# Moving modulation vectors, row transforms and magnitude products to other places in a state-space plus token-mixer kernel

## The chip, the cores and the metric

The kernel runs on one core of a Trainium2 chip. The metric is the device time of one execution in microseconds (us): median 664.15 us of three runs, from 663.93 to 666.26. The engines are named as the profile names them: PE is TensorE (PEld its weight loads), DVE is VectorE, ACT is ScalarE, POOL is GpSimd, and SP is SyncE, whose queue issues nearly all DMAs.

## The reference

The input x is a matrix of 2048 tokens by 448 channels. A conditioning vector gives six modulation vectors of 448 numbers, and the block then does two things with them.

```python
mod = (silu(c) @ w_mod).reshape(1, 6, 1, -1)         # sa, ca, ga, sb, cb, gb
h = layernorm(x) * (1 + ca) + sa
# S4D: K[d, l] = 2 Re sum_n C[d, n] exp(A[d, n] dt[d] l),  256 complex states per channel
y = irfft(rfft(h, 4096) * rfft(K, 4096))[:2048] + h * D_skip
x = x + ga * y
h = layernorm(x) * (1 + cb) + sb
# token mixer over the 2048 tokens, 1792 hidden
x = x + gb * (w2.T @ gelu(w1.T @ h + b1) + b2)
```

## The kernel before, in words

**The kernel table.** The first half of the program makes K. The 448 channels are 28 groups of 16, and each group takes two steps, so that `s` runs from 0 to 55. The steps stand in seven sets of eight. A set begins with a window (`window`, `late_window`), in which ACT has its exponential table loaded, and goes on with eight sine steps (`st_step`). In the window, round `e` of eight rounds has ACT take two exponentials (`st_exp`, tile `mag`) of what PE wrote (`st_exponents`, tiles `xe` and `xg`, two buffers each), while PE writes the exponents of the next step of the set. In a step, PE writes the phases of step s+1 (`st_phase`, the same tiles); ACT takes two absolute values and four sines; POOL makes the two halves of `G` (lines 737 and 738); DVE makes the four quarters of `E` (lines 739, 740, 742, 743). Two steps later PE multiplies `G` and `E` into `kg` (`st_kgen`, line 764). The second half of `E` needs a magnitude product `m` (`st_mag2`, a small product `w` on line 712 and a large one on line 717), made by POOL. In the sets that begin at steps 8, 16 and 24 the window makes two of these products and the steps make the other six.

**Work that rides along.** In the same half the input is normalized and transformed. `u_rows` (32 calls) multiplies rows of x by a table into `pu` (line 591), and DVE scales the result (line 595) into `yt`, whose DMA goes to DRAM. `u_cols` (16 calls) reads that back, multiplies again (line 627), and DVE writes `uo` (line 631), whose DMA writes `us_d`. `modulation(k, half)` makes vector k of the six: the first half is four products of the loaded `w_mod` columns (line 537), copied out as `parts`; the second half sums over partitions (line 533) and is copied out as `mod`. `chains` is a generator of the parameter logarithms and angles of the channel groups 1 to 3; `more(n)` advances it n steps. `st_s1` transforms finished kernel columns (`y`, line 802), and from step 33 on `piece` multiplies spectra (`kx`, `vv`). `warm(n)` and `idle(n)` issue n bf16 products whose result nobody reads.

**What sets the order.** PE, ACT, DVE and POOL follow the order in which the code is written. Two lists, `dve` and `act`, hold results that wait to be copied out; `flush` empties them. Inside a step, `between` empties `dve` between the second and the third quarter of `E`, so that results asked for in step s are copied out in the middle of step s+1. SP follows the code as well up to step 8 (`first`); from there on the scheduler puts its DMAs in order. A queue works strictly in its order.

**Buffers.** The small PSUM tiles of tag `ms` (`pu`, `pm`, `y`, `kx`, `vv`) share three buffers, `E` has three, `gs` three, `yt` three. Steps 32 to 55 reuse the memory of the pools that are closed at step 32 (`early.close()`), among them that of `uo`.

**The second half.** After step 55 the spectra of the other 224 channels are multiplied, then the layer norm and the token mixer follow, whose products are written as three products of split fp32r numbers (`acc`, lines 1400 to 1402; `o`, lines 1563 to 1565).

Of the kernel before, what the change touches and what calls it, by code (L numbers as in the profile page):

```python
# [22 lines left out]
P = 128  # L23
# [209 lines left out]
def tile_adaln_s4d_mixer(ctx, tc, i, out):  # L233
# [19 lines left out]
    with ExitStack() as es:  # L253
# [99 lines left out]
        def wm_slot(k):  # L353
# [8 lines left out]
                wm_load(0, wm_slot(0)),  # L362
# [8 lines left out]
            12: lambda: wm_load(4, xt[0:PP, 0:4, 0:D]),  # L371
            13: lambda: wm_load(5, xt[0:PP, 4:8, 0:D]),
            14: lambda: wm_load(3, xt[0:PP, 8:12, 0:D]),
        }

# [145 lines left out]
        scb = qp.tile([PP, 4, 32], F32, name="scb")  # L521
        sums = qp.tile([P, P], F32, name="sums")
# [6 lines left out]
        def modulation(k, half):  # L529

            pm = pms.tile([P, D], F32, tag="ms", name="pm")
            if half:
                T.matmul(pm, sums, pmods.pop(k), start=True, stop=True)
                act.append(lambda: S.activation(mod[k], pm, AF.Copy, bias=1.0 if k in (1, 4) else 0.0))
                return
            for q in range(4):
                T.matmul(pm[32 * q : 32 * q + 32], scb[:, q], wms[k][:, q], start=True, stop=True)
            pmods[k] = qp.tile([P, D], F32, tag="parts", name="parts")
            act.append(lambda: S.copy(pmods[k], pm))
# [29 lines left out]
        yts, wurs, lent = {}, {}, []  # L569
# [6 lines left out]
        def u_rows(n):  # L576

            R, g = divmod(n, 4)
            gp, gl = divmod(g, 2)
            if gl == 0:  # L580
                pair = n // 2
                if pair in (2, 4):
                    E = gp_.tile([P, 2, GD, NJ], F32, tag="E", name="yE")
                    rooms = E.rearrange("p a g j -> p (a g j)")[:, 0 : 4 * D].rearrange("p (h g d) -> p h g d", h=2, g=2)
                    lent.extend(rooms[:, h] for h in range(2))
                yts[R, gp] = lent[pair - 2] if 2 <= pair < 5 else xp.tile([P, 2, D], F32, tag="yt", name="yt", bufs=3)
            if g == 0 and R < 6:
                u_table(R + 2)
            pm = pms.tile([P, D], F32, tag="ms", name="pu")
            p = slice(64 * gl, 64 * gl + 64)  # L590
            T.matmul(pm, wurs[R][p, gp], xt[p, 2 * R + gp], start=True, stop=True)  # L591

            def out():
                mean = means[:, gl, 2 * R + gp : 2 * R + gp + 1]
                stt(yts[R, gp][:, gl], pm, mean, mod[1], ALU.add, ALU.mult)
# [46 lines left out]
        mags, m2s, eg, phs = {}, {}, {}, {}  # L642
# [66 lines left out]
        def st_mag2(s):  # L709
            me = v32(mags[s][:, 0])  # L710
            w = wp.tile([P, GD], F32, tag="w", name="w")
            G.tensor_tensor(w[:, :, None], me[:, :, 31:32], me[:, :, 1:2], ALU.mult)
            if s in (3, 4, 5):
# [3 lines left out]
            G.tensor_tensor(m2, me, w[:, :, None].to_broadcast([P, GD, 32]), ALU.mult)  # L717
            m2s[s] = m2
# [322 lines left out]
        def more(n):  # L1041

            for _ in range(n):
                if next(rest, None) in ("logs", "end"):
                    return
# [5 lines left out]
        def some(f, it, n):  # L1051
            for _ in range(n):
                k = next(it, None)
                if k is not None:
                    f(k)

# [15 lines left out]
        def late_window(s):  # L1072

            flush(hold)
            for e in range(BATCH):
# [10 lines left out]
                elif e in (3, 5):  # L1086
                    piece(False, True)
                st_mag2(s + e)
# [3 lines left out]
        def window(s):  # L1092
            if s:
                aside.append(True)
            angle()
# [9 lines left out]
            for e in range(BATCH):  # L1105
# [11 lines left out]
                if s < 32:  # L1117
                    more(WPACE[s // 8][e])
                if s == 0 and e >= 4:
                    u_stats(e - 4)  # L1120
                if s == 8 and e in (3, 4):
                    modulation(0, e - 3)
                if s == 8 and e == 5:
# [9 lines left out]
                for k, e0 in ((4, 1), (5, 3), (3, 6)) if s == 16 else ():  # L1133
                    if e in (e0, e0 + 1):
                        modulation(k, e - e0)
# [12 lines left out]
                elif s and (e < 2 or s >= 32):  # L1148
# [15 lines left out]
        WPACE = [[0, 2, 2, 1, 1, 1, 1, 1], [2, 2, 2, 2, 1, 3, 3, 1], [4] * 7 + [9], [4] * 8]  # L1164
        pace = [2] * 5 + [3, 4, 4] + [2] * 24
        for s in range(NHALF):
# [24 lines left out]
            def between():  # L1191
# [4 lines left out]
                if s < len(pace):  # L1196
# [3 lines left out]
            if True:  # L1200
                if s < 32 and s % BATCH > 1:
                    st_kgen(s - 2)
                if s % BATCH == 1 or s < 24 and s % BATCH == 0:
                    warm(10)
# [4 lines left out]
                if s == 7:  # L1209
                    warm(10)  # L1210

# [14 lines left out]
            if s in (1, 2):  # L1226
                x_load(4 + 4 * s, 4, G)
            if s in (23, 31):
# [3 lines left out]
            if s + 2 < 32 and (s + 2) % BATCH > 1 and s + 2 > 5:  # L1232
# [7 lines left out]
            if 8 <= s < 16 and free:  # L1240
                some(u_rows, rows, 2 if s % 2 else 3)
# [9 lines left out]
            if 17 <= s < 32 and free:  # L1251
                some(u_cols, cols, 1)
# [344 lines left out]
```

## Time and profile before

| what | value |
|---|---|
| median of three runs | 664.15 us (663.93 to 666.26) |
| the profiled execution | 663.85 us |
| its span in the trace | 662.1 us |
| busy in the span | PE 612.3, DVE 443.0, ACT 439.9, POOL 269.5 us |
| granted clock, mean | 0.984 |
| DMA | 123.67 MB, 187 GB/s |

The profiled execution spends 1.75 us outside its span and lies 0.30 us below the median. A timeline row gives start, duration, engine, line and tiles, and in brackets the idle time just before it with what ended that. A row of the table by stretches gives, behind the stretch and its length, the busy time of PE, PEld, DVE, ACT and POOL with the number of instructions, then the granted clock, the DMA share and GB/s.

### The profile page before, as it was taken

What the parts mean: (1) busy time and instruction counts of PE and PEld (TensorE: products, weight loads), DVE (VectorE), ACT (ScalarE), POOL (GpSimd) and SP (SyncE); (2) the same over time, 40 slices, a digit from 0 to 9 for tenths busy, and PEclk for the clock granted to TensorE, in tenths of its full rate; (3) what the DMA queues carried; (4) which work ended last, traced back from release to release, by engine and by line L of the source; (5) the groups of instructions that cost most, each with busy time, mean ns of one, the idle gap of its engine ahead of it and who ended that gap; (6) DMA issues with size and microseconds to landing.
All of it is one profiled execution on the core that took longest, in us unless ns stands there. A gap on an engine that the chain in (4) does not pass through costs nothing.

```text
span 662.1 us, 19161 instructions
## 1 busy us (share of the span) xinstructions
PE 612.3 (92%) x7639; PEld 442.9 (67%) x7639; DVE 443.0 (67%) x853; ACT 439.9 (66%) x828; POOL 269.5 (41%) x351
## 2 busy tenths in 40 slices
PE   1878998999999999999888999999999999999997
PEld 0444555445455565656544577788999999999996
DVE  8989889689894887868655688777422553333331
ACT  5978888899989999999587678885222522222220
POOL 7785597588599788787563000000000000000000
PEclk9998999989999999999999899999999999999999
DMA  6595747598775557576787999946755275555530
GB/s 145 156 219 166 253 143 257 182 248 268 218 247 178 103 166 218 169 215 182 234 274 227 257 247 234 233 112 196 201 160 153 57 209 164 162 160 166 161 106 28
DMA packets 97858, 123.67 MB, mean 187 GB/s; under 512 B 13717, under 2 KB 79801, under 8 KB 97769
## 3 DMA queue, kind: packets, MB, share of 16 engines
q1 hardware_dynamic: 97032, 120.02, 64.2%
q0 software_dynamic: 736, 2.43, 1.5%
q8 instruction: 60, 0.98, 0.7%
q14 instruction: 30, 0.24, 0.1%
HBM read 88.33 MB, written 33.59 MB: 184 GB/s over the span
## 4 chain that ended last, share of the span: by engine, by line
PE 63%; DMA 11%; DVE 9%; ACT 7%; POOL 4%; issue 4%; SPq 3%; ACTq 0%; DVEq 0%; POOLq 0%
PE o L1563 7%; PE o L1565 7%; PE o L1564 7%; PE acc L1400 6%; PE acc L1401 6%; PE acc L1402 6%; PE xe L667 6%; PE kg L764 6%; DMA w<-in_B_w_dram 3%; PE xg L667 3%; DMA xt<-in_A_u_dram 3%; DMA v_d<-vt 3%; PE pu L591 2%; PE vv L895 2%; PE kx L872 2%
## 5 line engine op out<-in xcount | busy, mean ns | idle before, releaser
L218 ACT CAST whi<-w 128x896 fp32r<-128x896 f32 x64 | 59.7, 939 | 138.5 <-PE o L1564 82.7
L227 DVE TENSOR_TENSOR wlo<-w,whi 128x896 fp32r<-128x896 f32 x64 | 68.1, 1086 | 41.4 <-ACT whi L218 35.1
L737 POOL TENSOR_TENSOR G<-mag,gs 128x512 f32<-128x512 f32 x56 | 71.9, 1283 | 36.4 <-ACT gs L733 36.4
L1400 PE MATMUL acc<-h3h,whi 128*128 128x448 f32 x224 | 83.0, 371 | 1.7 <-ACT h3h L1467 0.9
L1401 PE MATMUL acc<-h3l,whi 128*128 128x448 f32 x224 | 81.4, 363 | 0.5 <-DVE h3l L1474 0.3
L1563 PE MATMUL o<-uh,whi 128*128 128x448 f32 x224 | 81.3, 363 | 0.0
L1565 PE MATMUL o<-uh,wlo 128*128 128x448 f32 x224 | 81.2, 362 | 0.0
L1402 PE MATMUL acc<-h3h,wlo 128*128 128x448 f32 x224 | 81.0, 361 | 0.0
L1564 PE MATMUL o<-ul,whi 128*128 128x448 f32 x224 | 80.6, 360 | 0.0
L764 PEld LDWEIGHTS kg<-E,G 128*32 128x32 f32 x3584 | 56.2, 114 | 33.1 <-issue 18.4
L738 POOL TENSOR_TENSOR G<-mag,gs 128x512 f32<-128x512 f32 x56 | 71.9, 1285 | 0.0
L764 PE MATMUL kg<-E,G 128*32 128x64 f32 x3584 | 65.9, 227 | 6.4 <-issue 4.2
L667 PE MATMUL xg<-tab,lph 64*128 64x512 f32 x112 | 62.0, 553 | 6.6 <-DVE E L743 4.3
L1568 DVE TENSOR_TENSOR y<-o,x 128x448 f32<-128x448 f32 x16 | 10.0, 624 | 79.0 <-PE o L1565 79.0
L667 PE MATMUL xe<-tab,lph 64*128 64x512 f32 x112 | 61.9, 553 | 0.3 <-issue 0.2
L717 POOL TENSOR_TENSOR m<-mag,w 128x512 f32<-128x512 f32 x53 | 55.8, 1053 | 4.2
L1400 PEld LDWEIGHTS acc<-h3h,whi 128*128 128x128 f32 x224 | 42.0, 188 | 14.8 <-issue 2.1
L729 ACT ACTIVATE ab<-xe 128x512 f32<-128x512 f32 x56 | 33.9, 604 | 16.3 <-PE xg L667 9.1
L1401 PEld LDWEIGHTS acc<-h3l,whi 128*128 128x128 f32 x224 | 42.0, 187 | 3.8 <-DVE h3l L1474 0.9
L1565 PEld LDWEIGHTS o<-uh,wlo 128*128 128x128 f32 x224 | 42.1, 188 | 3.4
L1402 PEld LDWEIGHTS acc<-h3h,wlo 128*128 128x128 f32 x224 | 42.0, 187 | 3.1
L1564 PEld LDWEIGHTS o<-ul,whi 128*128 128x128 f32 x224 | 41.9, 187 | 3.0
(257 smaller groups left out, 1399.1 us busy)
## 6 DMA issues: line engine op xcount, KB each, us to landing
w<-in_B_w_dram SPq DMA_DIRECT2D x64, 224.0 KB
w<-in_B_w_dram SPq DMA_DIRECT2D x32, 448.0 KB
yi<-yu_d SPq DMA_DIRECT2D x32, 224.0 KB
us_d<-uo SPq DMA_DIRECT2D x16, 448.0 KB
u<-us_d SPq DMA_DIRECT2D x64, 112.0 KB
v_d<-vt SPq DMA_DIRECT2D x32, 224.0 KB
vt<-v_d SPq DMA_DIRECT2D x14, 448.0 KB
yu_d<-yt SPq DMA_DIRECT2D x13, 448.0 KB
```

The lines of the kernel that those rows point to most:

```text
L218: self.nc.scalar.copy(hi, w)
L227: eng.tensor_tensor(lo, w, hi.bitcast(F32), ALU.subtract)
L667: T.matmul(out[k], lhs[r], rhs[r], start=start, stop=stop)
L737: G.tensor_tensor(Gt[:, 1], mg_, v32(sg), ALU.mult)
L738: G.tensor_tensor(Gt[:, 0], mg_, v32(cg_), ALU.mult)
L764: T.matmul(kg[32 * q : 32 * q + 32, m], Gt[:, c, d], E[:, c, d], start=h == 0 and c == 0 and m == 0, stop=h == 1 and c == 1, skip_group_ch ...
L1400: nc.tensor.matmul(acc[f], hi[:, fs], h3h[:, r], start=r == 0, stop=False)
L1401: nc.tensor.matmul(acc[f], hi[:, fs], h3l[:, r], start=False, stop=False)
L1402: nc.tensor.matmul(acc[f], lo[:, fs], h3h[:, r], start=False, stop=r == 15)
L1563: nc.tensor.matmul(o, hi[:, ks], uh[kh][:, k], start=kh == 0 and k == 0, stop=False)
L1564: nc.tensor.matmul(o, hi[:, ks], ul[kh][:, k], start=False, stop=False)
L1565: nc.tensor.matmul(o, lo[:, ks], uh[kh][:, k], start=False, stop=kh == 1 and k == 6)
```

## The change

1. **Modulation vectors.** Vector 0 is made in the window at step 16 and no more in the one at step 8; vectors 4, 3 and 5 are made in the windows at steps 32, 40 and 48 (`last_mods`) and no more in the one at step 16. Results of these last three are copied out by DVE, not by ACT. Their `w_mod` columns are loaded into a lent `E` buffer after steps 31, 38 and 46 (`wm_room`).
2. **Rows.** `u_rows` takes two rows a step in steps 9 to 15 (it was three and two in turn from step 8 on), and the last eight rows in the window at step 16 (it was five). For later `yt` tiles, rows of x that are done with are lent (`spare`), and no `E` buffer.
3. **Copies behind E.** `at_once` puts the copies of `u_rows` and `u_cols` behind the fourth quarter of `E` of the same step.
4. **Magnitude products.** The windows at steps 8 and 16 make four instead of two (`MSET`); one lent `E` buffer holds two of them (`rooms`).
5. **Chains.** In steps 8 to 31 the chain is advanced at the end of a step. The window at step 16 does not begin the third chain; step 16 does.
6. **Warming.** The ten products after step 7's phases go, and step 9 has five for ten.

```diff
@@ modulation loads
-                wm_load(0, wm_slot(0)),
...
-            12: lambda: wm_load(4, xt[0:PP, 0:4, 0:D]),
-            13: lambda: wm_load(5, xt[0:PP, 4:8, 0:D]),
-            14: lambda: wm_load(3, xt[0:PP, 8:12, 0:D]),
+            12: lambda: wm_load(0, xt[0:PP, 0:4, 0:D]),
         }
+        def wm_room(k):
+            E = gp_.tile([P, 2, GD, NJ], F32, tag="E", name="wE")
+            wm_load(k, E.rearrange("p a g j -> p (a g j)")[0:PP, 0 : 4 * D].rearrange("p (q d) -> p q d", q=4))
+        last_mods = {32: 4, 40: 3, 48: 5}
@@ modulation
+                if k > 2:
+                    dve.append(lambda: ts(mod[k], pm, one_more, None, ALU.add))
...
+            (dve if k > 2 else act).append(lambda: (V.tensor_copy if k > 2 else S.copy)(parts, pm))
@@ new
+        def at_once(f, it, n):
+            k = len(dve)
+            some(f, it, n)
+            for out in dve[k:]:
+                out()
+            del dve[k:]
@@ late_window, e of eight
+                if e in (4, 6):
+                    modulation(last_mods[s], (e - 4) // 2)
@@ window
+            if s in (8, 16):
+                E = gp_.tile([P, 2, GD, NJ], F32, tag="E", name="mE")
+                for k in range(2):
+                    rooms[s + k] = E[:, k].rearrange("p g j -> p (g j)")[:, 0:512].rearrange("p (d i) -> p d i", i=32)
...
-                    more(WPACE[s // 8][e])
+                    more(WPACE[s // 8][e], s != 16)
...
-                if s == 8 and e in (3, 4):
-                    modulation(0, e - 3)
-                if s == 8 and e == 5:
+                if s == 16 and e == 4:
                     G.tensor_tensor(mod[0], mod[0], mod[2], ALU.mult)
...
-                for k, e0 in ((4, 1), (5, 3), (3, 6)) if s == 16 else ():
-                    if e in (e0, e0 + 1):
-                        modulation(k, e - e0)
+                if s == 16 and e in (1, 2):
+                    modulation(0, e - 1)
+                if s == 32 and e in (4, 6):
+                    modulation(last_mods[s], (e - 4) // 2)
...
-                elif s and (e < 2 or s >= 32):
+                elif s and e < (BATCH if s >= 32 else MSET[s // BATCH]):
                     st_mag2(s + e)
...
+        MSET = [0, 4, 4, 2]
@@ steps
-                if s < len(pace):
+                if s < len(pace) and not 8 <= s < 32:
                     more(pace[s])
...
-                    warm(10)
+                    warm(5 if s == 9 else 10)
...
-                if s == 7:
-                    warm(10)
...
+            if s in (31, 38, 46):
+                wm_room(last_mods[s + BATCH - s % BATCH])
...
-            if s + 2 < 32 and (s + 2) % BATCH > 1 and s + 2 > 5:
+            if s + 2 < 32 and (s + 2) % BATCH >= max(2, MSET[s // BATCH]) and s + 2 > 5:
                 st_mag2(s + 2)
...
-            if 8 <= s < 16 and free:
-                some(u_rows, rows, 2 if s % 2 else 3)
+            if 8 < s < 16 and free:
+                at_once(u_rows, rows, 2)
...
-                some(u_cols, cols, 1)
+                at_once(u_cols, cols, 1)
+            if 8 <= s < 32 and s % BATCH != BATCH - 1:
+                more(pace[s])
```

The first place is POOL from the middle of the window at step 8 into the first step of its set. Before:

```order
L404 CAST hl<-s 128x256
L784 TENSOR_TENSOR ks<-ks,dsk 128x8
L406 TENSOR_TENSOR hl<-s,hl 128x256
L574 TENSOR_TENSOR wur<-wu,rs 128x256
L1125 TENSOR_TENSOR mod_104<-mod_104,mod_106 128x448
L574 TENSOR_TENSOR wur<-wu,rs 128x256
L737 TENSOR_TENSOR G<-mag,gs 128x512
L738 TENSOR_TENSOR G<-mag,gs 128x512
L712 TENSOR_TENSOR w<-mag 128x16
L717 TENSOR_TENSOR m_1359<-mag,w 128x512
```

The same place on POOL after the change:

```order
L408 CAST hl<-s 128x256
L724 TENSOR_TENSOR w<-mag 128x16
L731 TENSOR_TENSOR m_1129<-mag,w 128x512
L798 TENSOR_TENSOR ks<-ks,dsk 128x8
L410 TENSOR_TENSOR hl<-s,hl 128x256
L587 TENSOR_TENSOR wur<-wu,rs 128x256
L724 TENSOR_TENSOR w<-mag 128x16
L731 TENSOR_TENSOR m_1153<-mag,w 128x512
L587 TENSOR_TENSOR wur<-wu,rs 128x256
L751 TENSOR_TENSOR G<-mag,gs 128x512
L752 TENSOR_TENSOR G<-mag,gs 128x512
L751 TENSOR_TENSOR G<-mag,gs 128x512
```

Two products `m` with their `w` stand ahead of the first `G` of the set, the product of `mod` is gone from here, and the `G` of the second step follows that of the first without a product between them.

The second place is SP around step 31, ahead of the window at step 32. `u` is what the first spectra read, `lph` are the phase rows of later groups. Before:

```order
L634 DMA us_d<-uo 128x2x448
L653 DMA lph_141<-pars_59 32x256
L634 DMA us_d<-uo 128x2x448
L657 DMA lph_141<-pars_59 64x1x256
L828 DMA u<-us_d 32x2x448 x4
L841 DMA si<-in_SI_dram 128x512
```

After the change:

```order
L646 DMA us_d<-uo 128x2x448
L665 DMA lph_141<-pars_59 32x256
L669 DMA lph_141<-pars_59 64x1x256
L665 DMA lph_139<-pars_59 32x256
L669 DMA lph_139<-pars_59 64x1x256
L842 DMA u<-us_d 32x2x448
L341 DMA wE<-in_w_mod_dram 112x4x448
L842 DMA u<-us_d 32x2x448 x3
L855 DMA si<-in_SI_dram 128x512
```

The load of vector 4's columns (`wE`) stands behind the first load of `u`, and one `us_d` fewer and one more pair of `lph` loads stand ahead of it.

The third place is PE in the later rounds of the window at step 32; `lex` are the exponents of the set, `lph` the phases of its first step. Before:

```order
L667 MATMUL xe<-tab,lex_144 128x512
L667 MATMUL xg<-tab,lex_144 128x512
L667 MATMUL xe<-tab,lex_145 128x512
L667 MATMUL xg<-tab,lex_145 128x512
L667 MATMUL xe<-tab,lex_145 128x512
L667 MATMUL xg<-tab,lex_145 128x512
L667 MATMUL xe<-tab,lph_140 128x512
L667 MATMUL xg<-tab,lph_140 128x512
```

After the change:

```order
L679 MATMUL xe<-tab,lex_144 128x512
L679 MATMUL xg<-tab,lex_144 128x512
L545 MATMUL pm<-wE,scb 32x448 x4
L679 MATMUL xe<-tab,lex_145 128x512
L679 MATMUL xg<-tab,lex_145 128x512
L679 MATMUL xe<-tab,lex_145 128x512
L679 MATMUL xg<-tab,lex_145 128x512
L537 MATMUL pm<-parts,sums 128x448
L679 MATMUL xe<-tab,lph_140 128x512
L679 MATMUL xg<-tab,lph_140 128x512
```

The product that needs `wE` stands ahead of the exponents of the set's last two steps and of the first phases; the sum stands between those exponents and the phases.

More of the change, by code (lines that the diff above doesn't have):

```diff
@@ L520, in tile_adaln_s4d_mixer @@
         sc = qp.tile([PP, 4], F32, name="sc")
-        scb = qp.tile([PP, 4, 32], F32, name="scb")
-        sums = qp.tile([P, P], F32, name="sums")
+        scb = cg.tile([PP, 4, 32], F32, name="scb")
+        sums = cg.tile([P, P], F32, name="sums")
         G.memset(sums, 0.0)
@@ L533, in modulation @@
                 T.matmul(pm, sums, pmods.pop(k), start=True, stop=True)
-                act.append(lambda: S.activation(mod[k], pm, AF.Copy, bias=1.0 if k in (1, 4) else 0.0))
+                one_more = 1.0 if k in (1, 4) else 0.0
+                if k > 2:
+                    dve.append(lambda: ts(mod[k], pm, one_more, None, ALU.add))
+                else:
+                    act.append(lambda: S.activation(mod[k], pm, AF.Copy, bias=one_more))
                 return
@@ L537, in modulation @@
                 T.matmul(pm[32 * q : 32 * q + 32], scb[:, q], wms[k][:, q], start=True, stop=True)
-            pmods[k] = qp.tile([P, D], F32, tag="parts", name="parts")
-            act.append(lambda: S.copy(pmods[k], pm))
+            if k > 2:
+                parts = wp.tile([P, 512], F32, tag="ab", name="parts", bufs=1)[:, 0:D]
+            else:
+                parts = qp.tile([P, D], F32, tag="parts", name="parts")
+            pmods[k] = parts
+            (dve if k > 2 else act).append(lambda: (V.tensor_copy if k > 2 else S.copy)(parts, pm))
         mv = xp.tile([P, 16, 2], F32, name="mv")
@@ L567, in u_means @@
             dve.append(lambda: V.tensor_copy(means, pm))
-        yts, wurs, lent = {}, {}, []
+        yts, wurs = {}, {}
+        spare = {3: 0, 4: 1, 6: 2, 8: 3, 10: 4, 12: 5, 14: 6}
         def u_table(R):
@@ L581, in u_rows @@
                 pair = n // 2
[L582 to L586, printed above, removed]
+                if pair in spare:
+                    yts[R, gp] = xt[:, 2 * spare[pair] : 2 * spare[pair] + 2]
+                else:
+                    yts[R, gp] = xp.tile([P, 2, D], F32, tag="yt", name="yt", bufs=3)
             if g == 0 and R < 6:
@@ L639, in u_cols @@
                 u_load(p + 4)
-        mags, m2s, eg, phs = {}, {}, {}, {}
+        mags, m2s, eg, phs, rooms = {}, {}, {}, {}, {}
         v32 = lambda t: t.rearrange("p (d i) -> p d i", i=32)
@@ L712, in st_mag2 @@
             G.tensor_tensor(w[:, :, None], me[:, :, 31:32], me[:, :, 1:2], ALU.mult)
-            if s in (3, 4, 5):
+            if s in rooms:
+                m2 = rooms.pop(s)
+            elif s in (3, 4, 5):
                 m2 = v32(wm0.rearrange("p k d -> p (k d)")[:, -512 * (s - 2) :][:, 0:512])
@@ L1039, in tile_adaln_s4d_mixer, with more @@
         rest = chains()
-        def more(n):
+        ended = [False]
+        def more(n, begin=True):
+            if ended[0] and not begin:
+                return
             for _ in range(n):
-                if next(rest, None) in ("logs", "end"):
+                at = next(rest, None)
+                ended[0] = at == "end"
+                if at in ("logs", "end"):
                     return
@@ L1160, in window @@
                 S.activation(one, one, AF.Sin)
-        WPACE = [[0, 2, 2, 1, 1, 1, 1, 1], [2, 2, 2, 2, 1, 3, 3, 1], [4] * 7 + [9], [4] * 8]
+        MSET = [0, 4, 4, 2]
+        WPACE = [[0, 2, 2, 1, 1, 1, 1, 1], [2, 2, 2, 2, 1, 3, 1, 3], [4] * 7 + [9], [4] * 8]
         pace = [2] * 5 + [3, 4, 4] + [2] * 24
```

## The prediction

> **What bounds the kernel now.** I read the page, then cut the span at the places where ACT's exponentials begin and end, and then read the timeline of the engine that is fullest in each stretch.
>
> In the table by stretches, behind the length stand the busy times of PE, PEld, DVE, ACT and POOL:
>
> ```profile
> 59.90:79.00 19.10, 16.91 (x257) 9.45 (x255) 16.37 (x35) 16.46 (x35) 10.84 (x18) 1.00 0.78 240
> 79.00:111.30 32.30, 29.96 (x561) 17.02 (x558) 28.72 (x50) 27.58 (x53) 27.57 (x31) 1.00 0.69 218
> 111.30:130.90 19.60, 18.08 (x319) 9.37 (x320) 13.90 (x29) 17.12 (x35) 10.20 (x17) 0.91 0.50 184
> 130.90:160.30 29.40, 28.14 (x515) 14.83 (x516) 26.53 (x47) 27.00 (x54) 25.30 (x28) 0.94 0.92 252
> 174.40:204.40 30.00, 27.85 (x606) 15.48 (x609) 27.70 (x47) 27.06 (x52) 27.06 (x32) 1.00 0.73 232
> 204.40:214.10 9.70, 9.29 (x198) 5.30 (x187) 2.21 (x4) 9.57 (x18) 9.17 (x15) 0.99 0.59 164
> 242.00:251.60 9.60, 9.57 (x155) 5.34 (x144) 5.35 (x11) 9.46 (x18) 8.74 (x15) 1.00 0.57 152
> ```
>
> The first two windows (59.90 and 111.30) leave ACT 2.5 us idle each, and PE has the most work. The sine sets at 79.00, 130.90 and 174.40 have four engines within 10 per cent of each other. In the windows at 204.40 and 242.00 ACT is full, and in that at 242.00 PE too. So work taken out of the early windows shortens them, and the same work put into the late ones has little room. Nothing behind step 55 is touched; it moves with the end of step 55.
>
> **The window at step 8.** It loses the modulation of vector 0 and, just ahead of it, ten warming products. The PE rows:
>
> ```profile
> 58.34 1.27 PE L679 MATMUL kg<-ones 128*128 128x256 bf16 x10
> ...
> 70.58 0.96 PE L537 MATMUL pm<-wm,scb 112*32 112x448 f32 x8
> 71.47 1.02 PE L591 MATMUL pu<-xt,wur 64*128 64x448 f32 x4
> ...
> 72.66 1.02 PE L533 MATMUL pm<-parts,sums 128*128 128x448 f32 x2
> 73.61 1.02 PE L591 MATMUL pu<-xt,wur 64*128 64x448 f32 x3
> ```
>
> From start to start, the two halves of a modulation hold PE for 0.89 (70.58 to 71.47) and 0.95 us (72.66 to 73.61), together 1.84 us. The timeline shows PE without idle time there, so I count all of it. The warming products delay ACT:
>
> ```profile
> 59.64 0.37 ACT L778 COPY ks<-kg 128x256 f32<-128x256 f32 x1 [1.38 <-PE kg L679]
> ```
>
> ACT gets back up to 1.38 us, but DVE, whose timeline has no gap here, paces what follows. I take half, 0.66 us; the bounds are 0 and 1.38. Together the window gives **2.5 us** (1.84 to 3.2). POOL's two added products lie in its 8 us of idle time, which is why they cost nothing; without that cover they would cost 2.6 us.
>
> **The set of steps 8 to 15.** The POOL groups:
>
> ```profile
> L738 POOL TENSOR_TENSOR G<-mag,gs 128x512 f32<-128x512 f32 x56 | 71.9, 1285 | 0.0
> L717 POOL TENSOR_TENSOR m<-mag,w 128x512 f32<-128x512 f32 x53 | 55.8, 1053 | 4.2
> L712 POOL TENSOR_TENSOR w<-mag 128x16 f32<-128x16 f32 x56 | 14.1, 253 | 2.4 <-ACT mag L696 1.5 <-DVE yk L808 0.8
> ```
>
> A step with a product takes POOL 2 x 1.28 + 1.05 + 0.25 = 3.9 us; POOL's timeline runs without a gap through steps 8 to 14, and ACT's next absolute value waits for a `gs` that POOL has to read. Two products fewer are 2 x 1.31 = 2.6 us. POOL's 27.57 busy us then fall to 25 beside ACT's 27.58, so POOL, now ahead, will wait for ACT in the first steps; I let 0.8 us be lost there. I take **1.8 us** (1 to 2.6). DVE loses three of fifteen rows:
>
> ```profile
> L595 DVE SCALAR_TENSOR_TENSOR yt<-pu,means,mod 128x448 f32<-128x448 f32 x22 | 14.0, 675 | 5.0 <-PE pu L591 3.5 <-DMA yu_d<-yt 1.5
> ```
>
> That is 2.0 us, and the lent rows of x end the 1.5 us wait for a `yt` on its way to DRAM. This does not shorten POOL's step, but DVE can end closer behind ACT, as the next rows need it (ACT's first logarithm step and first exponential, then DVE's first copy after the set's last `E`):
>
> ```profile
> 111.61 0.42 ACT L513 ACTIVATE xa<-ya 128x256 f32<-128x256 f32 x1
> ...
> 116.09 0.58 ACT L696 ACTIVATE mag<-xe 128x512 f32<-128x512 f32 x1
> ```
>
> ```profile
> 114.44 1.28 DVE L808 COPY yk<-y 128x512 f32<-128x512 f32 x2
> ```
>
> **The window at step 16.** Three modulations become one: 2 x 1.84 = 3.7 us less on PE. Three more rows come, at half of 1.02 us each: 1.5 us. That nets 2.2 us. PE's second exponents of the window wait for DVE's last `E`, done at 114.44, 2.8 us after ACT is (111.61). Of these 2.8 us I count 0.9, since ACT needs 4.5 us of logarithms (to 116.09) before it can use them. **3.1 us** (1.5 to 4).
>
> **The set of steps 16 to 23.** POOL again has two products fewer, but DVE gets the beginning of the third chain, which stood in the window's idle time:
>
> ```profile
> 131.18 0.29 DVE L457 TENSOR_TENSOR s<-xa,ya 128x128 f32<-128x128 f32 x1 [2.06 <-ACT ya L451]
> ...
> 133.49 0.29 DVE L470 SCALAR_TENSOR_TENSOR s<-t,s 128x128 f32<-128x128 f32 x1
> ```
>
> The seven operations take 2.6 us. DVE's busy 26.53 of 29.40 us leaves 2.9 us of waits, of which I let 2.0 be filled; **minus 0.6 us** (minus 2 to plus 1). At this point 2.5 + 1.8 + 3.1 - 0.6 = 6.8 us are won. In the set at 174.40 the products are as before, six, and moving the `uo` copies behind `E` changes neither POOL's nor DVE's sum; 0.
>
> **The window at step 32.** Here the load of vector 4 comes late. The SP rows before, and SP's longest wait there:
>
> ```profile
> 200.37 0.38 SPq L634 DMA_DIRECT2D us_d<-uo  x1
> ...
> 207.01 2.15 SPq L828 DMA_DIRECT2D u<-us_d  x4
> ```
>
> ```profile
> SPq L828 <- DMA us_d<-uo: 4.8, 1, 4.8
> ```
>
> The first `u` waits until the last `us_d` has landed, 6.6 us after its issue, and `wE` is queued behind that `u`. The last `us_d` now goes one place earlier, so I put the issue of `wE` at 206 on the old clock (205 to 207.6). How long does it fly? It has 784 KB. Nearest are a 256 KB load with 3.9 us, the 448 KB of `us_d` with 6.6, and the same columns earlier:
>
> ```profile
> tab<-in_TT_dram POOLq DMA_DIRECT2D x1, 256.0 KB, 3.9
> ```
>
> ```profile
> 43.96 0.33 SPq L341 DMA_DIRECT2D wm<-in_w_mod_dram  x1
> ```
>
> ```profile
> 54.91 0.96 PE L537 MATMUL pm<-wm,scb 112*32 112x448 f32 x8 [0.30 <-DMA wm<-in_w_mod_dram]
> ```
>
> That one took 10.9 us, behind a DMA backlog that I do not expect at 206 (DMA share 0.59 in the window's row). I take 6.3, near `us_d`, which had the same `lex` loads ahead of it: landing at 212.3. PE and ACT in the window:
>
> ```profile
> 210.62 0.50 PE L667 MATMUL xe<-tab,lex 64*128 64x512 f32 x1
> ```
>
> ```profile
> 211.87 0.65 ACT L696 ACTIVATE mag<-xe 128x512 f32<-128x512 f32 x1
> ```
>
> The product that needs `wE` would start at 210.6; behind it in PE's queue stand the exponents that ACT reads at 211.87, then the phases of step 32, so ACT waits for them. Stall 212.3 - 210.6 = 1.7 us. The 1.84 us of PE work itself costs about 0.5, since PE waits for ACT between rounds. **Minus 2.2 us** (0 to minus 6.8).
>
> **The windows at steps 40 and 48.** The loads have a set's time; only PE's 1.84 us count.
>
> ```profile
> 250.83 0.57 PE L667 MATMUL xe<-tab,lph 64*128 64x512 f32 x1
> ```
>
> ```profile
> 251.62 0.60 ACT L729 ACTIVATE ab<-xe 128x512 f32<-128x512 f32 x1
> ```
>
> The first half of the phases is whole at 250.83 + 0.57 = 251.40, and ACT takes it at 251.62. PE's slack is 0.2 us there; I allow 0.4 more for rounds in which PE waits for ACT, so 1.84 - 0.6 = 1.2 us each, **minus 2.4 us** (0 to minus 3.7). The two copies on DVE, 0.68 us each by the row above, lie beside its 4.2 idle us.
>
> **Sum.** 6.8 - 2.2 - 2.4 = 2.2 us. 663.85 - 2.2 = 661.65 for a profiled execution; plus the 0.3 us to the median, 662.0 us. Its own range is 660 to 664.5. A change under 0.5 per cent, 3.3 us, can hardly be told from none here.
>
> **The rivals.** *A, the late windows take the work.* If `wE` lands by 210.6, window 32 costs 0.5 and not 2.2 us, and if 40 and 48 behave like it, 0.45 each and not 1.2: 3.2 us better, 658.8 us (657.5 to 660.5). For it: the fast 3.9 us load. Against: PE 9.57 of 9.60 us.
>
> *B, PE's clock.* Warming goes, and a stalled PE idles. The granted clock already falls in the window at 111.30:
>
> ```profile
> 114.00:116.00 2.00, 1.71 (x34) 1.06 (x38) 2.00 (x4) 1.97 (x4) 0.00 (x0) 0.72 0.45 175
> 116.00:118.00 2.00, 2.00 (x48) 1.42 (x42) 0.48 (x2) 2.00 (x5) 1.59 (x4) 0.50 0.09 22
> 118.00:120.00 2.00, 2.00 (x74) 1.35 (x74) 1.30 (x3) 1.20 (x4) 0.98 (x1) 0.93 0.41 148
> ```
>
> Such a spell costs PE 0.28 x 2 + 0.5 x 2 + 0.07 x 2 = 1.7 us. Two more, ahead of step 8 and in window 32, make 662.0 + 3.4 = 665.4 us. [...]
>
> *C, slower.* The place is PE's wait for `wE` in window 32. If the load takes the 10.9 us of the row at 43.96, it lands at 216.9 and the window costs 6.8 us and not 2.2: 666.6 us; issued at 207, 667.6. It decides from a landing at 214.5, where the stall has eaten the 2.2 us.
>
> *D, the early gain fails.* If POOL and DVE hand over to a new wait in the set at step 8, that term is 0, 663.8 us. This lies in the forecast's own range.
>
> **Chances.** Forecast 0.50 (D in it), A 0.28, B 0.12, C 0.10. Faster by over 0.5 per cent, under 660.8: all of A and 0.06 of the forecast's lower edge, 0.34. Slower, over 667.5: 0.06 of C and 0.02 of B, 0.08. Within: 0.58. The range 657.8 to 666.4 leaves out the bottom of A and the top of C.
>
> **What would show it.** Right: the stretch at 59.90 is about 16.6 us long, that at 79.00 about 30.5, that at 111.30 about 16.5, that at 130.90 about 30; window 32 is 11.9 us with a PE wait for DMA `wE`, windows 40 and 48 are 10.8. POOL should show its gaps in steps 9 and 10. It is wrong if the early stretches do not shrink by 6 us together, if no row shows PE waiting for `wE`, or if the late windows keep 9.6 us.

## The result and the profile after

The changed kernel takes 688.55 us (median of four runs, 685.35 to 693.01), the kernel before 664.52 us beside it: ratio 1.036, interval 1.029 to 1.043. It is 24 us slower, where 2 us less was forecast. The profiled execution took 686.5 us, its span is 684.7 us (662.1 before): 22.6 us to be found.

I cut both traces at the starts of ACT's table loads, which open and close every window; the marks lie up to 1.2 us behind those of the prediction. The stretches of the changed kernel, with the same columns as there:

```profile
58.96:78.25 19.29, 16.28 (x246) 9.57 (x245) 18.35 (x37) 15.81 (x32) 13.69 (x23) 0.91 0.52 180
78.25:108.76 30.51, 26.84 (x588) 17.23 (x591) 29.59 (x52) 27.52 (x55) 25.55 (x28) 0.97 0.58 201
108.76:127.08 18.32, 17.09 (x292) 10.38 (x286) 13.95 (x25) 15.23 (x28) 12.12 (x20) 0.87 0.47 171
127.08:160.14 33.06, 27.65 (x506) 14.56 (x503) 30.04 (x51) 26.54 (x55) 25.60 (x27) 0.90 0.82 244
203.28:218.60 15.32, 12.22 (x273) 6.65 (x262) 3.49 (x7) 10.76 (x20) 12.13 (x19) 0.89 0.89 196
245.44:266.54 21.10, 16.29 (x226) 7.87 (x214) 6.64 (x14) 10.95 (x19) 11.89 (x19) 0.76 0.68 176
293.64:311.68 18.04, 13.14 (x226) 6.74 (x214) 6.64 (x14) 10.74 (x19) 11.88 (x19) 0.91 0.65 178
```

| stretch | before, us | after, us | difference | forecast |
|---|---|---|---|---|
| start to window 8 | 60.65 | 58.96 | -1.7 | |
| window 8 | 19.43 | 19.29 | -0.1 | -2.5 |
| steps 8 to 15 | 32.27 | 30.51 | -1.8 | -1.8 |
| window 16 | 19.72 | 18.32 | -1.4 | -3.1 |
| steps 16 to 23 | 29.00 | 33.06 | +4.1 | +0.6 |
| window 24 and its steps | 43.34 | 43.14 | -0.2 | 0 |
| window 32 | 10.82 | 15.32 | +4.5 | +2.2 |
| window 40 | 10.66 | 21.10 | +10.4 | +1.2 |
| window 48 | 10.66 | 18.04 | +7.4 | +1.2 |
| steps 32 to 39, 40 to 47, rest | 425.55 | 426.96 | +1.4 | 0 |

The first row is no gain: other kernels with the same code up to there reach window 8 between 58.05 and 60.73 us. Nearly the whole loss, 22.3 us, is in the three late windows. The same windows before:

```profile
204.41:215.23 10.82, 10.41 (x229) 6.15 (x222) 2.20 (x4) 10.66 (x21) 10.21 (x17) 0.94 0.63 170
242.06:252.72 10.66, 10.63 (x215) 6.30 (x203) 5.35 (x11) 10.52 (x19) 9.72 (x17) 1.00 0.58 151
280.02:290.68 10.66, 10.20 (x214) 6.09 (x202) 5.35 (x11) 10.61 (x19) 9.72 (x17) 1.00 0.68 190
```

In each of them ACT is busy for about 10.8 us (10.6 before), and stands idle for the rest. The list of waits of the whole program gives the reason, with sum, times and longest:

```profile
PE pm L545 <- DMA wE<-in_w_mod_dram: 10.7, 3, 4.1
```

Window 40, which loses most. SP's queue shows when the load goes out:

```profile
242.61 0.38 SPq L923 DMA_DIRECT2D v_d<-vt  x1
243.33 2.44 SPq L842 DMA_DIRECT2D u<-us_d  x4
247.10 0.36 SPq L855 DMA_DIRECT2D si<-in_SI_dram  x1
...
248.84 0.50 SPq L669 DMA_DIRECT2D lph<-pars  x1
249.54 0.32 SPq L341 DMA_DIRECT2D wE<-in_w_mod_dram  x1
```

`wE` was written behind step 38, but SP is later than the other engines, and seven loads stand between `v_d` and it: it leaves at 249.54, 4.1 us after the window has begun (245.44). Of the 6.9 us from `v_d` to `wE`, SP spends 4.1 on issuing and the rest on waiting. The chain of waits has the three flights, start and duration:

```profile
205.38 6.67 DMA wE<-in_w_mod_dram
...
249.54 8.34 DMA wE<-in_w_mod_dram
...
295.69 8.36 DMA wE<-in_w_mod_dram
```

PE's rows around the product that reads it, with one from window 48 to compare, then ACT's next exponential:

```profile
253.63 0.50 PE L679 MATMUL xg<-tab,lex 64*128 64x512 f32 x1
258.02 1.72 PE L545 MATMUL pm<-wE,scb 112*32 112x448 f32 x8 [3.89 <-DMA wE<-in_w_mod_dram]
...
260.39 1.77 PE L909 MATMUL vv<-z,si 64*64 64x224 f32 x16
...
298.66 0.99 PE L909 MATMUL vv<-z,si 64*64 64x224 f32 x16
```

```profile
260.55 0.60 ACT L708 ACTIVATE mag<-xe 128x512 f32<-128x512 f32 x1 [5.30 <-issue]
```

PE idles 3.89 us, and what follows is slow: the eight products take 1.72 us (0.96 in the prediction's row at 70.58), the sixteen `vv` 1.77 (0.99 at 298.66). Stretches of 2 us there:

```profile
255.00:257.00 2.00, 0.00 (x0) 0.00 (x0) 0.00 (x0) 0.25 (x1) 1.92 (x3) 0.97 1.06 219
257.00:259.00 2.00, 0.98 (x8) 0.23 (x8) 0.00 (x0) 0.00 (x0) 0.01 (x1) 0.50 0.66 167
...
261.00:263.00 2.00, 2.00 (x19) 0.79 (x12) 0.69 (x2) 0.66 (x3) 1.29 (x2) 0.50 0.14 45
```

The granted clock is 0.50 from about 1 us before the end of the wait until about 263.7. So each late load is paid twice: as a wait, and as work at half clock behind it. Over the three windows, (1 - clock) x length is 1.7 + 5.1 + 1.6 = 8.4 us, against 0.7 before. Not all of it follows a wait for a load. In window 40 the clock was at 0.50 once before, from about 250.0 to 253.4, and no idle time of PE in the window up to there is over 0.72 us:

```profile
249.00:251.00 2.00, 2.00 (x68) 1.53 (x67) 0.01 (x1) 1.09 (x2) 1.05 (x1) 0.76 0.51 115
251.00:253.00 2.00, 2.00 (x16) 1.09 (x20) 0.42 (x1) 1.28 (x3) 1.41 (x4) 0.50 0.97 277
```

That spell is 1.7 of the 8.4 us, and some 0.5 us more lie inside the wait, where a low clock costs nothing. About 6 us are left behind the three waits of 10.7 us. What began the early spell isn't known.

### The profile page after: what moved, and what is told of

The parts are those of the page before. It is cut to its first block, busy times and chain, and to the rows that moved or that the text cites. A ratio compares the mean times of both kernels' runs of the same rounds, so it can differ in the third digit from the quotient of the medians.

```text
span 684.7 us, 19112 instructions
## 1 busy us (share of the span) xinstructions
PE 614.2 (90%) x7624; PEld 444.6 (65%) x7624; DVE 453.3 (66%) x859; ACT 438.0 (64%) x822; POOL 271.0 (40%) x351
## 4 chain that ended last, share of the span: by engine, by line
PE 51%; DMA 17%; ACT 11%; DVE 8%; POOL 6%; issue 4%; SPq 2%; ACTq 0%; POOLq 0%; DVEq 0%
PE o L1600 7%; PE o L1599 7%; PE o L1601 6%; PE acc L1436 6%; PE acc L1437 6%; PE acc L1438 6%; DMA wE<-in_w_mod_dram 3%; PE xe L679 2%; DMA xt<-in_A_u_dram 2%; DMA lex<-pars 2%; POOL G L752 2%; PE kg L778 2%; DMA v_d<-vt 2%; DMA w<-in_B_w_dram 2%; POOL G L751 2%
## 5 line engine op out<-in xcount | busy, mean ns | idle before, releaser
L731 POOL TENSOR_TENSOR m<-mag,w 128x512 f32<-128x512 f32 x49 | 51.8, 1057 | 3.8
L708 ACT ACTIVATE mag<-xe 128x512 f32<-128x512 f32 x56 | 34.2, 611 | 23.6 <-issue 13.8
L1599 PEld LDWEIGHTS o<-uh,whi 128*128 128x128 f32 x224 | 42.0, 188 | 3.4
```

The source lines that it names most:

```text
L1599: nc.tensor.matmul(o, hi[:, ks], uh[kh][:, k], start=kh == 0 and k == 0, stop=False)
```

## The experiments

Theory 1: the loss is a load that SP issues too late, PE's wait for it in its in-order queue (in window 40 the exponents written behind the product start at 259.67, as it ends), and the low clock behind that wait. Rivals: the modulation's own work is what the windows can't hold (theory 2), or the lent `E` buffer (theory 3).

**Loads one step earlier.**

```diff
-            if s in (31, 38, 46):
+            if s in (30, 37, 45):
                 wm_room(last_mods[s + BATCH - s % BATCH])
```

> The changed kernel with one edit: the three loads into a lent E buffer are emitted one step earlier (behind the steps 30, 37 and 45 instead of 31, 38 and 46). In the queue of SP each then stands ahead of the u loads, about 3 us sooner for window 32 and 6 us sooner for 40 and 48. Theory 1 (the loss is the wait of TensorE, in order, for a load that SP issues only after the window has begun, and the low clock behind that wait): the wait of pm for the load, 10.7 us in three times, goes to under 1 us, the three windows fall from 15.3, 21.1 and 18.0 us to about 12, 11 and 11, and the time to 667 to 671 us. Theory 2 (the modulation's own matmuls and copies are what the windows can't hold): the wait goes but the windows stay above 13 us each, and the time is 677 to 681. Theory 3 (the lent E buffer stalls the steps next to the window): the time stays at 684 or more.

671.35 us (ratio 1.008, 1.005 to 1.010): 17 of the 24 us are back, which rules out theory 3, and theory 2 for most of the loss. The load for window 40 now leaves ahead of `u`; SP, then PE, then the clock after a wait that is left:

```profile
240.42 1.09 SPq L341 DMA_DIRECT2D wE<-in_w_mod_dram  x1
241.60 2.29 SPq L842 DMA_DIRECT2D u<-us_d  x4
```

```profile
250.06 0.96 PE L545 MATMUL pm<-wE,scb 112*32 112x448 f32 x8 [1.69 <-DMA wE<-in_w_mod_dram]
```

```profile
250.00:252.00 2.00, 1.94 (x22) 0.89 (x26) 0.62 (x1) 0.47 (x1) 1.92 (x3) 1.00 0.53 142
```

One wait of 1.69 us is left and the clock holds. The windows take 13.05, 13.91 and 12.92 us, 1 to 3 us more than theory 1 expected. That is 3.9 us over the windows without loads in the next run, and 3.8 of them are idle time of PE: this wait, and 1.36 and 0.71 us in the middle of the `kg` products of windows 32 and 48, for which the profile names no releaser ("issue").

**The products without the loads.**

```diff
-            E = gp_.tile([P, 2, GD, NJ], F32, tag="E", name="wE")
-            wm_load(k, E.rearrange(...))
+            wms[k] = tab.bitcast(F32)[0:PP, :, 0:D]
...
-                T.matmul(pm[32 * q : 32 * q + 32], scb[:, q], wms[k][:, q], start=True, stop=True)
+                T.matmul(pm[32 * q : 32 * q + 32], scb[:, q], wms[k][:, q % 3 if k > 2 else q], start=True, stop=True)
```

The three loads are left out; the products read a table that is in SBUF all the time, so that the vectors 3, 4 and 5 are not those of the block.

> The changed kernel without the three late loads: no E buffer is lent, and the first products of the modulations 3, 4 and 5 read a table that lies in SBUF all the time (so these three vectors hold wrong numbers; all instructions but the loads are there). Theory 1 (late load): 666 to 670 us, as with the early load or 1 us less. Theory 2 (the modulation's own work): 677 or more. Theory 3 (the lent buffer): 666 to 670 here, and over 680 with the early load.

667.56 us (1.003, 1.000 to 1.006). The three windows:

```profile
202.41:214.07 11.66, 11.14 (x272) 6.35 (x262) 3.48 (x7) 10.89 (x20) 11.03 (x18) 1.00 0.72 186
241.91:254.05 12.14, 12.13 (x226) 6.43 (x214) 6.64 (x14) 10.63 (x20) 11.13 (x19) 1.00 0.67 193
281.19:293.35 12.16, 12.12 (x226) 6.50 (x214) 6.63 (x14) 10.64 (x20) 11.14 (x19) 1.00 0.61 178
```

This is the price of a modulation's own work: 0.8, 1.5 and 1.5 us over the kernel before, 3.8 together, with PE full in the last two. Theory 2 holds for that much and no more. With the waits (10.7) and the clock (8.4; without the loads it stays at 1.00) it makes 22.9 us; 22.3 were lost. The 0.6 us too many are about the half clock inside the wait of window 40.

**No late modulations.**

```diff
-                if e in (4, 6):
-                    modulation(last_mods[s], (e - 4) // 2)
+            G.memset(mod[k], 0.5)        # k = 3, 4, 5, at the start
```

> The changed kernel without the modulations 3, 4 and 5 at all (their three vectors are set to 0.5 at the start): no load, no product, no copy in the windows 32, 40 and 48. All theories: the windows 32, 40 and 48 are as in the kernel before, 10.7 to 10.8 us each, and what is left is the effect of the other parts of the change without the work of three modulations: by the stages up to step 32 of the changed kernel (1.1 us ahead of the kernel before at the start of window 32) 663 to 667 us. Theory 1: 1 to 4 us under the runs with an early load or no load. Theory 2: over 10 us under them.

This kernel leaves the three vectors out. 664.30 us (0.999, 0.997 to 1.001), windows 40 and 48 at 10.66 and 10.65; window 32 took 11.65 us at clock 0.82, 0.9 us more than expected. So with three modulations less to compute, the rest of the change is no faster than the kernel before: the early gain of the forecast isn't there.

**This part alone, on the kernel before.** The edit is part 1 of the change for the vectors 3, 4 and 5.

> The kernel before with one part of the change alone: the modulations 4, 3 and 5 move from window 16 to the windows 32, 40 and 48, with their loads behind the steps 31, 38 and 46 into a lent E buffer, as the change has it; everything else is the kernel before. Theory 1: the whole loss of the late windows comes without any of the other parts: windows 32, 40 and 48 together over 45 us against 32 before, less 1 to 3 us saved in window 16: 678 to 688 us. A rival (the late windows only suffer because the other parts of the change put something else late ahead of them): under 672 us.

683.51 us (1.025, 1.021 to 1.030). Two early stretches, then the three late windows:

```profile
80.00:110.86 30.86, 29.83 (x560) 17.30 (x560) 28.80 (x50) 27.69 (x55) 27.94 (x31) 1.00 0.43 153
110.86:129.07 18.21, 17.26 (x314) 10.39 (x314) 14.26 (x31) 14.55 (x29) 9.63 (x17) 0.91 0.52 193
...
201.62:217.06 15.44, 13.37 (x273) 6.97 (x262) 3.48 (x7) 10.89 (x20) 12.21 (x19) 0.78 0.83 209
...
243.88:264.86 20.98, 14.96 (x226) 7.41 (x221) 6.63 (x14) 10.84 (x19) 11.91 (x19) 0.84 0.68 177
...
291.94:310.07 18.13, 13.55 (x226) 6.80 (x214) 6.64 (x14) 10.74 (x20) 11.87 (x19) 0.91 0.74 190
```

The late windows take 54.6 us together, as in the changed kernel (54.5), so the loss needs no other part. The way there differs in window 32: here `wE` left at 199.55, ahead of `u`, and PE did not wait for it. PE stood idle in the middle of the `kg` products, for which the profile names no releaser, and the clock was 0.50 from about 207.6 to 214.4 (an estimate: the exponents' rows take 0.79 us there for 0.50, and the window's mean is 0.78):

```profile
206.84 0.90 PE L776 MATMUL kg<-E,G 128*32 128x64 f32 x47 [1.75 <-issue]
```

Gaps of this kind of 0.71 to 1.75 us stand in the late windows of three kernels that load into lent `E` buffers (1.36 and 0.71 with the early loads, 1.75 and 0.77 here, 1.23 in the run with two magnitude products); that the loads make them isn't shown. And this part alone takes steps 8 to 15 from 32.3 to 30.9 us (its loads have left; DMA share 0.43 for 0.68) and window 16 from 19.7 to 18.2.

**One other part undone at a time**, each on the kernel with the early loads (671.35 us). The chain:

```diff
-                    more(WPACE[s // 8][e], s != 16)
+                    more(WPACE[s // 8][e])
...
-                if s < len(pace) and not 8 <= s < 32:
+                if s < len(pace):
                     more(pace[s])
...
-            if 8 <= s < 32 and s % BATCH != BATCH - 1:
-                more(pace[s])
```

> The changed kernel with the early loads (671.4 us), with the part on the chain undone: the chain's steps stand between the two products of E again, as in the kernel before, and the third chain begins in window 16. Theory 1 (a chain step that stands beside POOL's products is slow on DVE, 0.8 to 1.3 us in place of 0.2 to 0.5, and the third chain's seven steps in the steps 16 to 18 cost the set 16 to 23 what window 16 saves): set 16 to 23 falls by 1 to 2 us, window 16 rises by 1 to 2, sum within 1 us of 671.4. Theory 2 (the chain part is the one that holds the set back): 669 or less. Theory 3 (it pays, as forecast): 672.5 or more.

673.83 us (1.013, 1.010 to 1.017). Against the run with the early loads window 16 rises by 2.8 to 22.1 us and its steps fall by 2.3 to 28.3, the way theory 1 says and by more, +0.6 us in sum. Steps 8 to 15 rise by 2.1 to 32.6, which theory 1 left out. The median is theory 3's, that the part pays as a whole; but its interval overlaps with that of the run with the early loads (1.005 to 1.010), and of the two profiled executions this one is the faster, by 1 us. So the stages show it and the whole does not. The timelines of this run and of the changed kernel show what its place in the steps costs. DVE in the changed kernel, in steps 17 and 18, POOL at the same time, and then the same operations in this run, at the end of window 16 and just behind it, where POOL is idle (132.20 to 136.19):

```profile
137.88 0.78 DVE L465 TENSOR_SCALAR s<-s 128x128 f32<-128x128 f32 x1
...
143.15 1.02 DVE L469 TENSOR_TENSOR ya<-ya,xa 128x128 f32<-128x128 f32 x1
144.10 1.30 DVE L472 TENSOR_SCALAR t<-s 128x128 f32<-128x128 f32 x1
```

```profile
137.30 1.28 POOL L752 TENSOR_TENSOR G<-mag,gs 128x512 f32<-128x512 f32 x1
...
142.75 1.28 POOL L751 TENSOR_TENSOR G<-mag,gs 128x512 f32<-128x512 f32 x1 [2.84 <-ACT gs L747]
143.99 1.33 POOL L752 TENSOR_TENSOR G<-mag,gs 128x512 f32<-128x512 f32 x1
```

```profile
133.38 0.22 DVE L465 TENSOR_SCALAR s<-s 128x128 f32<-128x128 f32 x1
...
134.69 0.29 DVE L469 TENSOR_TENSOR ya<-ya,xa 128x128 f32<-128x128 f32 x1
134.90 0.22 DVE L472 TENSOR_SCALAR t<-s 128x128 f32<-128x128 f32 x1
```

All seven operations of the third chain's beginning take 5.2 us in the steps and 2.55 there. A slow one ends 0.1 us or so after POOL's product does (138.66 after 138.58; 144.17 after 144.03; 145.40 after 145.32).

The magnitude products (`MSET = [0, 2, 2, 2]`, no lent `mE`), and the copies behind `E` (`some` for `at_once`):

> The changed kernel with the early loads (671.4 us), with two magnitude products in the windows 8 and 16 instead of four, and no E buffer lent for them: the other two stand in the steps behind again. Theory 1 (POOL is what ends the steps of the sets 8 to 15 and 16 to 23, so that two products fewer are worth their 1.3 us each): 673 to 674 us. Theory 2 (what was saved in the steps was paid in the windows): 671 to 672. Theory 3 (the lent E buffer and POOL's work in the windows slow them): under 670.

670.76 us (1.010, 1.006 to 1.014).

> The changed kernel with the early loads (671.4 us), with the rows' and columns' copies between the two halves of E again instead of behind the second half. Theory 1 (DVE's order around the row copies decides when E is whole, as forecast; worth 0.1 us a step): 672 to 673. Theory 2 (a copy that stands at the end of a step makes DVE wait for pu in the set 16 to 23, where the first columns wait for their load): 669 to 670.5. Theory 3 (DVE isn't what ends a step): 671 to 672, no difference.

671.17 us (1.011, 1.007 to 1.014). Neither can be told from 671.35; both fit only "what was saved in one place was paid in another" or no effect. The first is blurred by a load that was late again in its profiled execution, the slowest of six (674.45): window 32 took 17.18 us there, 13.05 in the run that it is compared with.

The filling products back (`warm(10)` behind step 7 and in step 9):

> The changed kernel with the early loads (671.4 us), with the filling matmuls put back: ten behind step 7, ten instead of five in step 9. Theory 1 (without them TensorE stands idle long enough at the start of window 8 that its granted clock falls: 0.91 in window 8 in three of four profiles of kernels without them, 1.00 in both kernels with them, 1.7 us): granted clock 1.00 in window 8, 669.5 to 671. Theory 2 (the clock spell only moves, since the next idle stretch brings one anyway): 671 to 672. Theory 3 (the filling is work in the way, as the change has it): 672 or more.

677.46 us (1.019, 1.016 to 1.021): the time is theory 3's. Window 8 is the shortest of all runs, 18.27 us, and its clock is 1.00, as theory 1 expected; but the run with the early loads had 18.35 at 0.91, so the clock won next to nothing there. And 6 us are lost elsewhere, in the profiled execution mostly in steps 32 to 39 (29.25 us at 0.88) and window 48 (17.10 at 0.80), where PE met another late load:

```profile
291.28 1.76 PE L886 MATMUL kx<-yk,si 128*64 128x224 f32 x8 [3.39 <-DMA u<-us_d]
```

The early `wE` now stands ahead of `u`, and here `u` was the late one. That the filling caused this isn't shown.

**Part 1 undone**, the other five kept but for three of the seven lent rows of x, which the loads need; the modulations are called at their old places again:

```diff
+                wm_load(0, wm_slot(0)),
...
-            12: lambda: wm_load(0, xt[0:PP, 0:4, 0:D]),
+            12: lambda: wm_load(4, xt[0:PP, 0:4, 0:D]),
+            13: lambda: wm_load(5, xt[0:PP, 4:8, 0:D]),
+            14: lambda: wm_load(3, xt[0:PP, 8:12, 0:D]),
...
-        spare = {3: 0, 4: 1, 6: 2, 8: 3, 10: 4, 12: 5, 14: 6}
+        spare = {3: 0, 4: 1, 6: 2, 8: 3}
```

> The changed kernel with the first part undone: the modulation 0 is in window 8 again, 4, 5 and 3 in window 16, with their loads at the steps 7, 12, 13 and 14 (only four of the seven borrowed xt rows are left to the row products, since the loads need the others). Theory 1 (the late load alone made the loss; the other parts together are worth little): 663 to 667 us. A rival (the other parts are worth the 5 us and more that the forecast gave to the early windows, and moving the modulations cost all of it): under 660. Another (they lose by themselves): over 668.

674.99 us (1.013, 1.007 to 1.018), in the range of "they lose by themselves". But this was no clean undoing: with two rows a step, the rows of x that the load at step 14 overwrites aren't all used by then (one row pair is computed from overwritten rows), and PE waits:

```profile
PE pu L600 <- DMA xt<-in_w_mod_dram: 7.2, 1, 7.2
```

So the load was put at step 16 (`16:` for `14:`):

> The changed kernel with the first part undone, and the load of modulation 3 issued at step 16 instead of 14, after the row products have read the xt rows that it overwrites (in the run before, TensorE waited 7.2 us in set 8 to 15 for that load, and one row pair was computed from overwritten rows). Theory 1 (the other parts together are worth nothing): 664 to 668 us. Rival (they are worth 5 us and more): under 660. Rival (they lose by themselves, by rows moved into window 16): 668 to 671.

667.12 us (1.003, 1.000 to 1.005), as theory 1 has it. The other five parts together lose 1.7 us (0.3 to 3.2) and gain nothing like 5.

**Modulations in steps, not in windows**, loaded 3 to 8 steps ahead into columns of `yk1` that are not yet written:

```diff
+            if s in mod_at:      # {36: (4, 0), 38: (4, 1), 42: (3, 0), 44: (3, 1), 50: (5, 0), 52: (5, 1)}
+                modulation(*mod_at[s])
+            if s in room_at:     # {33: 4, 34: 3, 42: 5}
+                wm_room(room_at[s])
```

> The kernel before, with the modulations 4, 3 and 5 moved in another way: loaded behind the steps 33, 34 and 42 into columns of yk1 that are still unused, their products behind the steps 36 to 52 where ACT ends the steps and TensorE has some 0.2 to 0.3 us a step to spare, none in a window. Theory 1 (work that is there in time and beside a busy ACT costs nothing; what leaves the set 8 to 15 and window 16, 1.4 and 1.5 us in the run with that part alone, is kept): 661 to 663 us. Theory 2 (the products' own time, 1.4 us each on TensorE, is paid wherever they stand): 665 to 667. [...]

On the kernel before: 665.44 us (1.001, 0.997 to 1.005), which is theory 2's time. The late windows hardly pay any more; together they take 33.0 us, against 32.1 before and 54.6 above. In the profiled execution all from window 32 on takes 1.7 us more than before, not the 4 us that theory 2 gives three modulations. Window 8 took 22.2 us at clock 0.85 there, so the 3 us won in steps 8 to 15 and window 16 don't show.

> The changed kernel with the modulations 4, 3 and 5 loaded into columns of yk1 and multiplied behind the steps 36 to 52, as in the run on the kernel before. Theory 1: as fast as the changed kernel without these modulations or 1 us over it, 663.5 to 666 us, the windows 32, 40 and 48 at 10.7 to 11.7 us. Theory 2 (products paid wherever they stand): 667 to 669.

On the changed kernel: 668.06 us (1.004, 1.001 to 1.008), theory 2's time again. But its runs spread from 663.9 to 672.4, over both theories, and the profiled one (663.93) is among the fastest.

**What the other parts lose.** With the old number of rows a step (`2 if s % 2 else 3`, from step 8) on the kernel of the last run:

> The changed kernel with the modulations 4, 3 and 5 behind the steps 36 to 52 (668.1 us), and with the old number of row products a step, three and two in turn from step 8 on, instead of two from step 9 on. Theory A (the rows that the change leaves to window 16 hold TensorE there, and make the yi loads and the first columns late): window 16 and set 16 to 23 together fall from 49.8 us to 47.5 or less, set 8 to 15 rises by under 1, and the time is 665 to 666.5. Theory B (DVE and the low clock set these stages, not the rows): window 16 and its set stay at 49 or more, and the time at 668 or above.

666.20 us (1.001, 0.998 to 1.003), 2 us less and theory A's time; the intervals overlap, and the profiled executions stand the other way (666.47 and 663.93), so a gain isn't shown. Window 16 fell from 19.25 to 17.28 us, but steps 8 to 15 rose by 1.6 and steps 16 to 23 by 0.7. Neither theory's whole pattern came.

The four magnitude products in window 8 alone, on the kernel before with modulations in steps:

> The kernel before with the modulations 4, 3 and 5 behind the steps 36 to 52 (665.4 us), and four magnitude products in window 8 in place of two, the two more in a lent E buffer. Theory A (POOL ends the steps 8 and 9, as forecast): 663 to 664. Theory B (the steps take the same time, since DVE or TensorE is next): 665 to 666.

670.72 us (1.008, 1.005 to 1.011), 5 us slower than the same kernel with two products in window 8, for a reason that neither theory has. In that kernel two `E` buffers are lent to rows as well:

```profile
DVE E L757 <- DMA yu_d<-yE: 4.6, 2, 3.4
```

With a third one lent to magnitudes, DVE waits for a lent buffer's DMA before it can write `E`, which it did not with two products; steps 8 to 15 take 34.3 us, 3.5 more.

No version beats the kernel before: the best, with 0.999, leaves out work.

## Why the prediction was wrong, point by point

- **The step that failed** is "The loads have a set's time; only PE's 1.84 us count", on the windows 40 and 48. Their loads stand behind the steps 38 and 46, with one step between them and the window and not a set, in a queue that runs late: they left 4.1 and 2.1 us after the window had begun and flew 8.3 and 8.4 us, and PE waited 3.9 and 4.1 us for them. Forecast +2.4 us, measured +17.8. Without the loads the two windows take 3.0 us more than before. That `wE` could land late was a rival (C), but only for window 32, the one of the three that lost least.
- **Window 32** was reasoned rightly. Issue 205.4 us, which is 206.5 on the old clock (forecast 206), flight 6.7 (6.3), wait 10.7 - 3.9 - 4.1 = 2.7 us (1.7). It cost 4.5 us and not 2.2: 1.0 more of waiting, 0.3 more of work, and the clock behind the wait (1.7 against 0.7 before), which was not in the sum. In the run of part 1 alone the same window took as long (15.4) without any wait for `wE`, so this cost can come another way.
- **PE's clock** (rival B, at 1.7 us a spell) had both its spells, in the windows 8 and 32, and at that size, though the first cost little (see below). It did not have the windows 40 and 48; with them the clock is 8.4 us, of which some 6 stand behind the waits. I set it aside since no gap over 2 us was expected; that a shorter one leaves the clock alone was an estimate of mine, and no run shows such a limit. The waits of 4.1, 3.9, 3.4 and 2.7 us above were each followed by 0.50, but so was one of 1.67 us (two magnitude products), while one of 1.69 us left the clock at 1.00 (early loads), and at 250.0 it fell with no idle time over 0.72 us before it in the window.
- **The work itself**: 1.2 us a window forecast for 40 and 48, 1.5 measured without the loads; 0.5 for window 32, 0.8 measured. Nearly right in size.
- **The early gain** is the second term that failed: from the start of window 8 to that of window 32 the changed kernel takes 144.3 us against 143.8 before, 0.6 more where 6.8 less was forecast. The next points take it apart; what eats it is in part open.
- **Steps 8 to 15**, -1.8 forecast, -1.8 measured. POOL shows the gaps in steps 9 and 10 that the forecast named (1.28 and 0.90 us). But the number is partly luck: part 1 on the kernel before gives -1.4 by itself, part 1 undone also leaves 30.1 us, so the gains overlap, and the run without the loads, with the same code up to there, took 32.1.
- **Window 8** and **window 16** gave 0.1 and 1.4 us for 2.5 and 3.1. In window 8 the clock was 0.91, but that does not explain it: the same code took 18.35 us at 0.91 (early loads) and 18.85 at 1.00 (no loads), and 18.27 at 1.00 with the filling put back. What sets it isn't known. In window 16, part 1 alone gives 1.5, so the other parts give nothing there; four other runs of the same code took 19.2 to 19.3 us at 0.82. The rows moved there may be why: with the old number it took 17.3.
- **Steps 16 to 23**, +0.6 forecast, +4.1 measured. The chain's seven operations were costed at 2.6 us from rows in a window; beside POOL they take 5.2. In the changed kernel PE also waits for `yi` with the first columns, and the clock is at 0.50 for some 7 us (134.0 to 140.8), so that ACT stands idle:

```profile
134.83 1.77 PE L639 MATMUL pu<-yi,s 64*64 64x448 f32 x6 [0.90 <-DMA yi<-yu_d]
```

```profile
140.58 0.60 ACT L743 ACTIVATE ab<-xe 128x512 f32<-128x512 f32 x1 [3.58 <-PE xg L679]
```

  Other kernels with the same code there take 30.6 us at clock 0.94 (early loads, no loads) or 32.7 at 0.90 (no modulations); which of them comes seems to hang on that spell. What starts it isn't settled.
- **Rival D** said that the early gain fails, but looked for it in the wrong place: the set at step 8 kept its 1.8 us, and the windows 8 and 16 and the steps 16 to 23 did not give what was forecast. It was priced at no loss beyond that one term.

## What to carry to other kernels

A load that is moved must be followed to its landing in every place, on the queue that issues it: count what stands ahead of it there, and how far that queue is behind, not the steps in the code. Work on an in-order engine that waits for a load belongs where it holds up nothing, well after the load: 3 to 8 steps were enough here. If it is late, add the clock to the price of the wait, here some 6 us behind 10.7 us of waits. And an operation's time is taken from a row with the same neighbour: what runs beside POOL is not what runs alone (5.2 us for 2.55 here).

## What the runs showed of the hardware

- DVE's 128x128 `tensor_scalar` and `tensor_tensor` on SBUF took 0.22 to 0.29 us with POOL idle (chain undone) and 0.49 to 1.30 us with a POOL product under way (changed kernel, 131.71 to 145.40), and ended 0.08 to 0.15 us after it. The `E` products, which read one side from PSUM, took 0.67 to 0.69 us in the changed kernel, beside a POOL product (130.51 to 131.79) and with POOL idle (140.18 to 142.05). Why the two kinds differ isn't shown.
- An idle PE is not always punished: a wait of 1.69 us left the clock at 1.00 (early loads, window 40), the 1.75 us of idling in the run of part 1 alone (by its rows, 0.79 us for 0.50) and a wait of 1.67 us in the run with two magnitude products were followed by 0.50. In the last, PE had stood idle for some 3.3 us of the 5.7 up to the wait's end (1.23, 0.45 and 1.67); in the first it was full until the wait (2.00 us of each 2.00 from 244 to 248). PE's row and a stretch of the last run:

```profile
211.58 1.72 PE L545 MATMUL pm<-wE,scb 112*32 112x448 f32 x8 [1.67 <-DMA wE<-in_w_mod_dram]
```

```profile
213.00:215.00 2.00, 2.00 (x9) 1.00 (x6) 0.62 (x1) 0.89 (x2) 0.28 (x2) 0.50 0.62 187
```

- The three loads of 784 KB in the changed kernel flew 6.7 to 8.4 us, with a DMA share of 0.91 to 1.11 for most of each flight (in stretches of 2 us). With the early loads, the one for window 40 took 9.6 us from issue to the end of PE's wait (240.42 to 250.06).
